# Three of eight feature pairs of the first MLP product by seven block products instead of eight, in chunks 2 to 5

## The chip, the cores and the metric

The kernel runs on one core of a Trainium2 chip. The metric is the device time of one execution in microseconds (us). A core has a matrix engine (TensorE, "PE" in the profile, its weight loads "PEld"), a vector engine (VectorE, "DVE"), a scalar engine (ScalarE, "ACT"), GpSimd ("POOL") and a queue engine for transfers (SyncE, "SP"). Each engine takes its own instructions in order, and they wait for each other by semaphores.

## What is computed

The input is a delta-rule attention over 4 batches, 8 heads, 768 tokens and 48 dimensions per head, followed by an MLP with a SiLU over 3072 tokens of 384 features.

```python
k_n = k / (np.linalg.norm(k, axis=-1, keepdims=True) + 1e-06)
for t in range(S):
    y[:, :, t] = np.einsum('bhd,bhde->bhe', q[:, :, t], state)
    v_old = np.einsum('bhde,bhd->bhe', state, kt)
    state = state + bt[:, :, :, None] * np.einsum('bhd,bhe->bhde', kt, vt - v_old)
...
x = attn_out.transpose(0, 2, 1, 3).reshape(B * S, H * D)
h = x @ w_in                       # 3072x384 by 384x2048
g = h * (1.0 / (1.0 + np.exp(-h)))
return g @ w_out                   # 3072x2048 by 2048x384
```

## The kernel before

The sequence is cut into six chunks of 128 tokens, numbered c = 0 to 5, and each chunk into two halves (hf = 0, 1) of 64 tokens. For each chunk the attention part needs the inverse of a triangular block of 32x32 per head (`invert`, a loop of 31 rank-1 steps on DVE, two instructions each), some small products on PE (`merge`, `keys`, `inner`, `old`, `new`, `update`), and copies by ACT and DVE. The result of a half chunk, transposed, is `xT[c, hf]`: 384 features as three blocks of 128 partitions, by 256 tokens (64 tokens of 4 batches).

For each half chunk the MLP then runs two stages. `hidden` makes the first product: the 2048 hidden features are 16 blocks of 128, taken as eight pairs f = 0 to 7. For one pair, six matmuls of 128x128 weights by 256 tokens fill one bank of PSUM (two feature blocks of 256 tokens, three matmuls accumulating into each), and ACT writes the SiLU of that bank to SBUF (`gT`, L1039, 128x512). The matmuls are in fp32, and every one of them is two MATMUL records and two LDWEIGHTS records in the profile. Two banks, `m0` and `m1`, are used in turn (`bank(M, "phid")`). `combine` makes the second product, in chunks 1 to 5 by seven block products instead of eight, with sums of blocks of `gT` that DVE makes (`sum_g`, L1118), and 192 columns to a matmul (L1136).

The order of the work is written out by hand. The generators `feed_forward(c, hf)` hand out the MLP in small steps, and `run(n)` puts n of these steps between the steps of the attention part; `pin` keeps every engine in the order in which instructions were written. So the PE's queue has matmuls of the MLP between the small products, and DVE's queue has `sum_g` between the rank-1 steps. While `invert(c + 1, ...)` is being written, three of four rank-1 steps are followed by one step of the MLP:

```python
for n, _ in enumerate(invert(c + 1, step)):
    run(int(n % 4 != 3 and n != 24))
```

In chunks 2, 3 and 4 these steps fall on `combine(c, 0)` and `hidden(c, 1)`. In chunk 5 there is no inverse to make for a next chunk. After `invert` come the sums of squares of the chunk after the next (`lengths`, L377, of squares that POOL makes) and the steps of its norms (L391 to L421), still with steps of the MLP between. `hidden` gives a step after three matmuls and one after six, so 16 steps to a half chunk.

Lines that the prediction uses: L1029 the matmuls of the first product, L1039 its SiLU, L1136 those of the second product, L1118 `sum_g`, L615 and L620 the two instructions of a rank-1 step, L623 the scaling at the end of `invert`, L535 a copy by DVE, L532 a copy by ACT, L527 a mask that DVE multiplies onto a score in PSUM, L1144 a scaling by ACT.

Of the kernel before, what the change touches and what calls it, by code (L numbers as in the profile page):

```python
# [10 lines left out]
FP32 = mybir.dt.float32  # L11
U32 = mybir.dt.uint32
ACTF = mybir.ActivationFunctionType
ALU = mybir.AluOpType
# [5 lines left out]
def kernel(  # L20
# [22 lines left out]
    NKT = DM // P  # L43
    NFF = DFF // P
    HB = B // 2
    HH = HB * H
    GT = B * W
    FG = 3
# [55 lines left out]
    def go(steps, n=1):  # L104
        for _ in range(n):
            next(steps, None)
# [9 lines left out]

    kbufs = [const.tile([P, B, NP, 2, W], FP32, name=f"kb{s}") for s in range(2)]
    zbuf = const.tile([P, B, 2, NP, W], FP32, name="z")
    vfs = {}
    LO, HI = slice(0, W), slice(W, P)  # L120
    HALVES = (LO, HI)

    def on(e, hf, g):

        return HALVES[hf ^ e ^ g]

    sums_of_g = const.tile([P, 2, NFF // 2, C], FP32, name="sums_of_g")
# [17 lines left out]
    RUN = C // T * D  # L145
    stage = const.tile([P, B * NP * 2 * C], FP32, name="stage")
# [16 lines left out]
    def in_blocks(c):  # L163

        return 1 < c < NCH
# [7 lines left out]

    def load_k(c, bs=ALL):
        if c < NCH:
            load_pair(kbufs[c % 2], k, c, bs)

    def load_q(c, bs=ALL):
        if c < NCH:
# [25 lines left out]
    for e in range(2):  # L205
        for g in range(2):
            to, of = slice(HH * e + HH // 2 * g, HH * e + HH // 2 * (g + 1)), slice(HH // 2 * g, HH // 2 * (g + 1))
# [6 lines left out]
    w_in = const.tile([P, NKT, DFF], FP32, name="w_in")  # L214
# [83 lines left out]
    def narrow_w_out(i):  # L298
# [14 lines left out]
        out=above[0:W], in_=above[0:W], pattern=[[1, W]], compare_op=ALU.is_gt, fill=0.0,  # L313
# [3 lines left out]
        out=above[W:P], in_=above[W:P], pattern=[[1, W]], compare_op=ALU.is_gt, fill=0.0,  # L317
# [5 lines left out]
    for j in range(NB):  # L323
        rows = slice(T * j, T * (j + 1))
# [36 lines left out]
    def square(c, b):  # L361

        if b == 0:
            sums[c] = small.tile([P, BH], FP32, name="ss", bufs=1)[:]
        if c > 2:
            squared[c, b] = zbuf[:, b].rearrange("p s a w -> p (s a) w")[:, :, 0:D]
        elif b % HB == 0:
            tag = "g" if c > 0 or b > 0 else "x"
            both = work.tile([P, HB, H, D], FP32, name="sq", tag=tag, bufs=1)
            for u in range(HB):  # L370
                squared[c, b + u] = both[:, u]
        kb = kbufs[c % 2][:, b].rearrange("p a e w -> p (a e) w")[:, :, 0:D]
        pin(nc.gpsimd.tensor_tensor(out=squared[c, b], in0=kb, in1=kb, op=ALU.mult))

    def add_squares(c, b):
# [155 lines left out]
    def by_act(to, of):  # L531
        return pin(nc.scalar.copy(to, of))  # L532
# [219 lines left out]
    xTs, parts = {}, {}  # L752
# [88 lines left out]
    def update(c, g, hf):  # L841

        if c == NCH - 1 and hf == 1:
            return
        pu = bank(CC, "pu")
        for u, p, e, n, of, _ in of_heads():
            rows = on(e, hf, g)
            yield pin(nc.tensor.matmul(  # L848
                pu[of, n * D : (n + 1) * D], lhsT=kbufs[c % 2][rows, g * HB + u, p, e, 0:D],
                rhs=zbuf[rows, g * HB + u, hf, p, 0:D], start=True, stop=True,  # L850
            ))
        to = states[g][:, :, :, 0:D]
        pin(nc.vector.tensor_tensor(out=to, in0=to, in1=by_heads(pu), op=ALU.add))
# [160 lines left out]
    gTs = {}  # L1014

    def hidden_of(c, hf, f):

        if (c, hf) == (0, 1):
            return turned_kq[:].rearrange("p b j a t -> p (b j a t)")[:, f * 2 * GT : (f + 1) * 2 * GT]
        return gTs[f // FG][:, f % FG, :]  # L1020

    def hidden(c, hf):

        for f in range(NFF // 2):
            assert ("in", f) in narrowed
            ph = bank(M, "phid")
            for j in range(2):
                for a in range(NKT):
                    pin(nc.tensor.matmul(  # L1029
                        ph[:, j * GT : (j + 1) * GT],  # L1030
                        lhsT=w_in[:, a, (2 * f + j) * P : (2 * f + j + 1) * P],
                        rhs=xTs[c, hf][:, a, :],
                        start=(a == 0), stop=(a == NKT - 1),
                    ))
                if j == 0:
                    yield
            if f % FG == 0 and (c, hf) != (0, 1):
                gTs[f // FG] = mlp.tile([P, FG, 2 * GT], FP32, name="gT", bufs=3)
            pin(nc.scalar.activation(  # L1039
                out=hidden_of(c, hf, f), in_=ph[:], func=ACTF.Silu, scale=-0.5 if in_blocks(c) else 0.5  # L1040
            ))
            if c > 0 and f % FG == 1 and f >= FG:
                for which in (S1, S2):
                    sum_g(which, f // FG - 1)
            yield
# [41 lines left out]
    def sum_w():  # L1087
# [14 lines left out]
    S1, S2, S3, S4 = (  # L1102
        (0, (0, 1), (1, 1), ALU.add), (1, 0, (0, 0), ALU.subtract),
        (0, (0, 0), (0, 1), ALU.subtract), (1, (1, 0), 1, ALU.subtract),
    )

    def group(g):
        return slice(FG * g, min(FG * (g + 1), NFF // 2))

    def sum_g(which, g):  # L1110
        k, left, right, op = which
        fs = group(g)
        of = [
            sums_of_g[:, x, fs] if isinstance(x, int) else
            gTs[g][:, 0 : fs.stop - fs.start, x[0] * GT + x[1] * C : x[0] * GT + (x[1] + 1) * C]
            for x in (left, right)
        ]
        pin(nc.vector.tensor_tensor(out=sums_of_g[:, k, fs], in0=of[0], in1=of[1], op=op))  # L1118
# [251 lines left out]
    def run(n=1):  # L1370

        for _ in range(n):
            name = next(needed, None)
            if name is not None:
                until(name)
            go(pieces)
            begin_soon()
# [121 lines left out]
    for c in range(1, NCH):  # L1499
        if c > 1:  # L1500
            solving = solve(c)
            for n in range(9):
                go(solving)
                run((2, 2, 2, 2, 1, 1, 2, 2, 2)[n])
                if n == 5:
                    pieces = chained(pieces, feed_forward(c, 0), feed_forward(c, 1))
        assert next(solving, 0) == 0
        go(long_2, 99)
        if c + 1 < NCH:
            ready = prepare(c + 1)  # L1510
# [48 lines left out]
```

## Time and profile before

| | us |
|---|---|
| three runs | 653.5, 654.77, 656.47 (median 654.77) |
| the profiled execution | 652.37, its span 650.4 |
| PE busy | 627.6 (96% of the span) |
| DVE busy | 397.6 (61%) |
| ACT busy | 213.8 (33%) |
| POOL busy | 90.9 (14%) |
| mean granted TensorE clock | 0.990 |

A row of the profile names the source line, the engine, the operation, what is written and read, the shapes (partitions x elements) and the count; then the busy time of the group and the mean duration of one, and last the idle time of the engine just before, with what ended it. "Idle time" of PE is counted from the modelled end of one matmul to the start of the next; matmuls overlap in the pipe, so a busy PE may still have lost time, and the distance between the starts of neighbouring matmuls says more than the busy share.

### The profile page before, as it was taken

What the parts mean: (1) busy time and instruction counts of PE and PEld (TensorE: products, weight loads), DVE (VectorE), ACT (ScalarE), POOL (GpSimd) and SP (SyncE); (2) the same over time, 40 slices, a digit from 0 to 9 for tenths busy, and PEclk for the clock granted to TensorE, in tenths of its full rate; (3) what the DMA queues carried; (4) which work ended last, traced back from release to release, by engine and by line L of the source; (5) the groups of instructions that cost most, each with busy time, mean ns of one, the idle gap of its engine ahead of it and who ended that gap; (6) DMA issues with size and microseconds to landing.
All of it is one profiled execution on the core that took longest, in us unless ns stands there. A gap on an engine that the chain in (4) does not pass through costs nothing.

```text
span 650.4 us, 21395 instructions
## 1 busy us (share of the span) xinstructions
PE 627.6 (96%) x9416; PEld 548.0 (84%) x9416; DVE 397.6 (61%) x911; ACT 213.8 (33%) x497; POOL 90.9 (14%) x92
## 2 busy tenths in 40 slices
PE   7878899999989999999999999999999999999997
PEld 5577778756779989989989989989989989889997
DVE  5875689997764987453986453987454974103112
ACT  2455663332342122451122452122451122451111
POOL 5023631334101020010020010020011000000000
PEclk9979999999989999999999999999999999999999
DMA  9876534250288324268324268324173024100101
GB/s 136 209 165 206 192 75 104 98 97 3 53 154 148 58 73 60 50 136 143 59 76 57 48 131 146 61 74 60 28 153 72 10 65 60 40 13 1 25 0 25
DMA packets 145676, 54.70 MB, mean 84 GB/s; under 512 B 117152, under 2 KB 138912, under 8 KB 145584
## 3 DMA queue, kind: packets, MB, share of 16 engines
q1 hardware_dynamic: 143136, 52.93, 39.6%
q8 instruction: 74, 1.21, 0.8%
q10 hardware_dynamic: 2448, 0.41, 0.4%
q14 instruction: 18, 0.15, 0.1%
HBM read 40.14 MB, written 11.01 MB: 79 GB/s over the span
## 4 chain that ended last, share of the span: by engine, by line
PE 91%; DMA 2%; issue 2%; DVE 2%; ACT 1%; SPq 1%; DVEq 0%
PE phid L1029 38%; PE px L1136 16%; PE py L1136 12%; PE po L1064 5%; PE pb_c L828 3%; PE pa L517 2%; PE pb_c L816 2%; PE pyc L907 2%; PE pb_c L1064 2%; PE pb_c L848 1%; PE pb_c L336 1%; PE pyc L894 1%; DMA kb<-in_k_dram 1%; PE pt L488 1%; PE py L770 1%
## 5 line engine op out<-in xcount | busy, mean ns | idle before, releaser
L1029 PE MATMUL phid<-xT,w_in 128*128 128x256 f32 x1152 | 260.1, 383 | 2.1 <-DMA xT<-part 2.0
L1029 PEld LDWEIGHTS phid<-xT,w_in 128*128 128x128 f32 x1152 | 216.9, 191 | 34.4 <-issue 3.0
L1039 ACT ACTIVATE gT<-phid 128x512 f32<-128x512 f32 x88 | 52.5, 597 | 149.8 <-PE phid L1029 145.2
L615 DVE SCALAR_TENSOR_TENSOR rank<-g,step,x 128x31 f32<-128x31 f32 (+15 forms) x124 | 49.8, 401 | 35.8 <-DMA g<-blocks 32.3
L1118 DVE TENSOR_TENSOR sums_of_g<-gT 128x384 f32<-128x384 f32 (+1 forms) x60 | 29.9, 518 | 59.0 <-ACT gT L1039 48.4
L1136 PE MATMUL py<-w_out,sums_of_g 128*128 128x192 f32 x320 | 56.8, 329 | 0.0
L1136 PE MATMUL px<-sums_of_w,sums_of_g 128*128 128x192 f32 x320 | 56.8, 329 | 0.0
L1136 PEld LDWEIGHTS px<-sums_of_w,sums_of_g 128*128 128x128 f32 x320 | 52.2, 190 | 0.5
L1136 PEld LDWEIGHTS py<-w_out,sums_of_g 128*128 128x128 f32 x320 | 52.2, 190 | 0.4
L620 DVE TENSOR_TENSOR x<-x,rank 128x31 f32<-128x31 f32 (+15 forms) x124 | 42.5, 343 | 4.3
L455 POOL TENSOR_TENSOR vf<-vf,n_slot 128x768 f32<-128x768 f32 x10 | 15.0, 1516 | 169.3 <-DMA vf<-in_v_dram 125.3
L476 DVE STREAM_TRANSPOSE kq<-stage 128x512 f32<-128x512 f32 x28 | 28.5, 1114 | 12.0 <-DMA stage<-in_q_dram 10.4
L532 ACT COPY xT<-pyc 48x128 f32<-48x128 f32 (+2 forms) x126 | 32.6, 259 | 1.6
L1136 PE MATMUL px<-sums_of_w,gT 128*128 128x192 f32 x160 | 28.4, 329 | 0.0
L1136 PE MATMUL py<-w_out,gT 128*128 128x192 f32 x160 | 28.4, 329 | 0.0
L1136 PE MATMUL px<-w_out,gT 128*128 128x192 f32 x160 | 28.0, 327 | 0.0
L1136 PEld LDWEIGHTS px<-w_out,gT 128*128 128x128 f32 x160 | 26.4, 190 | 0.5
L538 POOL COPY g<-x 64x256 f32<-64x256 f32 x4 | 5.0, 1241 | 154.5 <-DVE x L623 154.5
L1136 PEld LDWEIGHTS py<-w_out,gT 128*128 128x128 f32 x160 | 26.1, 190 | 0.3
L1136 PEld LDWEIGHTS px<-sums_of_w,gT 128*128 128x128 f32 x160 | 26.1, 190 | 0.2
L828 PEld LDWEIGHTS pb_c<-vf,xi 64*64 64x64 f32 x736 | 23.5, 138 | 3.2 <-issue 2.9
L1147 DVE TENSOR_TENSOR o<-o,kept 128x192 f32<-128x192 f32 (+1 forms) x29 | 11.5, 422 | 24.0 <-ACT kept L1144 24.0
(221 smaller groups left out, 921.6 us busy)
## 6 DMA issues: line engine op xcount, KB each, us to landing
vf<-in_v_dram SPq DMA_DIRECT2D x48, 96.0 KB, 3.2
out_dram<-o SPq DMA_DIRECT2D x42, 96.0 KB, 2.2
w_out<-in_moe_w_in_dram SPq DMA_DIRECT2D x4, 768.0 KB, 4.4
sums_of_w<-in_moe_w_out_dram SPq DMA_DIRECT2D x4, 768.0 KB, 5.9
blocks<-ap SPq DMA_DIRECT2D x44, 64.0 KB, 1.9
g<-blocks SPq DMA_DIRECT2D x5, 512.0 KB, 3.5
kb<-in_k_dram SPq DMA_DIRECT2D x12, 192.0 KB, 5.1
kb<-in_k_dram SPq DMA_DIRECT2D x24, 96.0 KB, 4.6
```

The lines of the kernel that those rows point to most:

```text
L455: pin(nc.gpsimd.tensor_tensor(out=vf, in0=vf, in1=of, op=ALU.mult))
L476: pin(nc.vector.transpose(out=kqs[c, b][:, :, j, :].rearrange("p a (i m) -> p a m i", i=T), in_=src.rearrange("p a (m d) -> p a m d", d=D) ...
L517: pin(nc.tensor.matmul(pa[e][half, p * n * W : (p + 1) * n * W], lhsT=kq[rows, p, 0, half], rhs=kq[rows, p, js[0] : js[-1] + 1, half], sta ...
L532: return pin(nc.scalar.copy(to, of))
L615: pin(nc.vector.scalar_tensor_tensor(out=tv, in0=g[:, 0:m, m : m + 1].to_broadcast([P, m, n]), scalar=step[:, m : m + 1], in1=x[:, m : m + ...
L620: yield pin(nc.vector.tensor_tensor(out=x[:, 0:m, m:T], in0=x[:, 0:m, m:T], in1=tv, op=ALU.add))
L828: yield pin(nc.tensor.matmul(pz[rows, n * D : (n + 1) * D], lhsT=xis[g][rows, u * H + 2 * p + e, :], rhs=vfs[c][rows, hf, g * HB + u, p, : ...
L1029: pin(nc.tensor.matmul(ph[:, j * GT : (j + 1) * GT], lhsT=w_in[:, a, (2 * f + j) * P : (2 * f + j + 1) * P], rhs=xTs[c, hf][:, a, :], star ...
L1039: pin(nc.scalar.activation(out=hidden_of(c, hf, f), in_=ph[:], func=ACTF.Silu, scale=-0.5 if in_blocks(c) else 0.5))
L1064: pin(nc.tensor.matmul(pos[i][:, 0:DM], lhsT=hidden_of(0, hf, f // 2)[:, at : at + C], rhs=w_outs[f // HFF][:, f % HFF, :], start=(f == 0) ...
L1118: pin(nc.vector.tensor_tensor(out=sums_of_g[:, k, fs], in0=of[0], in1=of[1], op=op))
L1136: pin(nc.tensor.matmul(to, lhsT=at, rhs=quarter(f, *b) if isinstance(b, tuple) else sums_of_w[b][:, f], start=start and f == 0, stop=f == ...
```

## The change

It concerns `hidden` for chunks 2 to 5 alone. There, pairs f = 1, 3 and 5 are made by seven block products for eight. A pair has two feature blocks (j = 0, 1), and the 256 tokens are two blocks of 128; over two of the three row blocks (feature blocks a = 0 and 1 of `xT`) this is a 2x2 by 2x2 product of 128x128 blocks, and it is made with seven products of sums of blocks. The third row block (a = 2) is made with four plain products, into which the shared sums are accumulated. That gives eleven matmuls of 128 columns to such a pair, in five groups (`product_steps`: 4, 3, 1, 1 and 2 matmuls), in place of six of 256.

The sums of weight blocks (`w1` to `w4`) are made once, by five DVE instructions in chunk 2 (`sums_of_blocks`), and stay in SBUF. Room for them comes from the tail of `stage` and from the tail of the second key buffer, whose rows are packed without gaps in chunks 3 and 5 (`keys_of`). The sums of token blocks (`x1` to `x5`) are made by four DVE instructions in each half chunk (`add_x`, one of 256 columns and three of 128).

Within a pair by seven, three regions of 128 columns of one PSUM bank, `a`, `b` and `d`, are used: ACT copies `b` and `d` out after the first group, DVE adds `a` to the first of these copies after the second group and ACT copies `d` again, DVE adds `a` again after the third and the fourth group, and after the fifth ACT makes the SiLU of `a` (128 columns) and of the three other blocks (384 columns). Each matmul that follows in `a` accumulates onto what stands there. Between the groups stand matmuls of a plain pair (f + 1), which uses the other bank: one after the first group, two between the second and the third, one between the third and the fourth, one between the fourth and the fifth, one after the fifth.

In the order of the built program, a wait on PSUM goes by bank: the copy of `d` waits for the addition that reads `a`, and the next matmul into `a` waits for that copy; the first matmul of the second group waits for the copy of `b` and `d`. The order on SP and POOL is the same in both programs, and so is the number of steps that `hidden` gives (16).

```diff
+    by_seven = (1, 3, 5)
...
+    def sums_of_blocks():
...
+        a11, a12, a21, a22 = (of(a, j, 0, NS) for j, a in ((0, 0), (0, 1), (1, 0), (1, 1)))
+        pin(nc.vector.scalar_tensor_tensor(
+            out=w1, in0=a21, scalar=-1.0, in1=a22, op0=ALU.mult, op1=ALU.subtract
+        ))
...
+    def hidden_by_seven(c, hf):
...
+        def plain(f):
+
+            ph = bank(M, "phid")
+            for j in range(2):
+                for a in range(NKT):
+                    w = w_in[:, a, (2 * f + j) * P : (2 * f + j + 1) * P]
+                    mm(ph[:, j * GT : (j + 1) * GT], w, xT[:, a, :], a == 0, a == NKT - 1)
+                    yield
+            silu(hidden_of(c, hf, f), ph[:])
+
+        def product_steps(f):
+
+            i = by_seven.index(f)
+            ph, to = bank(M, "phid"), hidden_of(c, hf, f)
+            a, b, d = ph[:, 0:C], ph[:, C : 2 * C], ph[:, 2 * C : 3 * C]
+            at_11, at_22, at_21 = to[:, C : 2 * C], to[:, 2 * C : 3 * C], to[:, 3 * C : 4 * C]
+            mm(d, w3[:, i], x3, start=True)
+            mm(d, w_block(i, 2, 1), x(2, 1))
+            mm(b, w_block(i, 1, 0), x(1, 0))
+            mm(b, w_block(i, 2, 0), x(2, 0), stop=True)
+            by_act(to[:, C : 3 * C], ph[:, C : 3 * C])
+            yield
+            mm(a, w_block(i, 0, 0), x(0, 0))
+            mm(d, w_block(i, 1, 1), x4)
+            mm(d, w_block(i, 2, 1), x5, stop=True)
+            add_x(at_11, a, at_11, ALU.add)
+            by_act(at_21, d)
+            yield
+            mm(a, w2[:, i], x2)
+            add_x(at_21, a, at_21, ALU.add)
+            yield
+            mm(a, w1[:, i], x1)
+            add_x(at_22, a, at_22, ALU.add)
+            yield
+            mm(a, w4(i), x(1, 1))
+            mm(a, w_block(i, 2, 0), x(2, 1), stop=True)
+            silu(to[:, 0:C], a)
+            silu(to[:, C:], to[:, C:])
+            yield
+
+        differ = free[:, 0 : 2 * C].rearrange("p (n t) -> p n t", t=C)
+        first = plain(0)
+        go(first, 3)
+        add_x(differ, xT[:, 0::2, C : 2 * C], xT[:, 0::2, 0:C], ALU.subtract)
+        add_x(x3, x(1, 1), x(0, 1), ALU.subtract)
+        add_x(x2, x(1, 1), x1, ALU.add)
+        add_x(x4, x(1, 0), x2, ALU.subtract)
+        yield
+        go(first, 99)
+        yield
+        for n, f in enumerate(by_seven):
+            by, beside = product_steps(f), plain(f + 1)
+            go(by)
+            go(beside)
+            yield
+            go(by)
+            go(beside)
+            yield
+            go(beside)
+            go(by)
+            go(beside)
+            go(by)
+            yield
+            go(beside)
+            go(by)
+            go(beside, 99)
+            if n == 1:
+                for which in (S1, S2):
+                    sum_g(which, 0)
+            yield
+        last = plain(NFF // 2 - 1)
...
     def hidden(c, hf):
 
+        if in_blocks(c):
+            yield from hidden_by_seven(c, hf)
+            return
...
+                if c == 2 and n == 3:
+                    sums_of_blocks()
```

More of the change, by code (lines that the diff above doesn't have):

```diff
@@ L118, with keys_of @@
     zbuf = const.tile([P, B, 2, NP, W], FP32, name="z")
+    KEPT = B * H * D
+    def keys_of(c):
+        if c % 2 == 0 or c == 1:
+            return kbufs[c % 2]
+        flat = kbufs[1][:].rearrange("p b a e w -> p (b a e w)")
+        return flat[:, 0:KEPT].rearrange("p (b a e d) -> p b a e d", b=B, a=NP, e=2)
     vfs = {}
@@ L175, in load_k @@
         if c < NCH:
-            load_pair(kbufs[c % 2], k, c, bs)
+            load_pair(keys_of(c), k, c, bs)
     def load_q(c, bs=ALL):
@@ L371, in square @@
                 squared[c, b + u] = both[:, u]
-        kb = kbufs[c % 2][:, b].rearrange("p a e w -> p (a e) w")[:, :, 0:D]
+        kb = keys_of(c)[:, b].rearrange("p a e w -> p (a e) w")[:, :, 0:D]
         pin(nc.gpsimd.tensor_tensor(out=squared[c, b], in0=kb, in1=kb, op=ALU.mult))
@@ L848, in update @@
             yield pin(nc.tensor.matmul(
-                pu[of, n * D : (n + 1) * D], lhsT=kbufs[c % 2][rows, g * HB + u, p, e, 0:D],
+                pu[of, n * D : (n + 1) * D], lhsT=keys_of(c)[rows, g * HB + u, p, e, 0:D],
                 rhs=zbuf[rows, g * HB + u, hf, p, 0:D], start=True, stop=True,
@@ L1020, in hidden_of, with blocks_of @@
         return gTs[f // FG][:, f % FG, :]
+    by_seven = (1, 3, 5)
+    NS = len(by_seven)
+    tail = stage[:, B * NP * RUN :]
+    key_tail = kbufs[1][:].rearrange("p b a e w -> p (b a e w)")[:, KEPT:]
+    assert NS * P + P <= B * H * (W - D) and 2 * NS * P + 2 * P <= B * NP * (2 * C - RUN)
+    def blocks_of(t, at, n=NS):
+        return t[:, P * at : P * (at + n)].rearrange("p (n m) -> p n m", m=P)
+    w1, w2, w3 = blocks_of(tail, 0), blocks_of(key_tail, 0), blocks_of(tail, NS)
+    w4s = [blocks_of(tail, 2 * NS, 2), blocks_of(key_tail, NS, 1)]
@@ new lines, in w_block, with of @@
+    def w_block(i, a, j):
+        f = by_seven[i]
+        return w_in[:, a, (2 * f + j) * P : (2 * f + j + 1) * P]
+    def sums_of_blocks():
+        def of(a, j, i, n):
+            span = w_in[:, a, 2 * P : 2 * P + 4 * P * NS].rearrange("p (i q m) -> p i q m", q=4, m=P)
+            return span[:, i : i + n, j]
+        a11, a12, a21, a22 = (of(a, j, 0, NS) for j, a in ((0, 0), (0, 1), (1, 0), (1, 1)))
+        pin(nc.vector.scalar_tensor_tensor(
+            out=w1, in0=a21, scalar=-1.0, in1=a22, op0=ALU.mult, op1=ALU.subtract
+        ))
+        pin(nc.vector.scalar_tensor_tensor(
+            out=w2, in0=w1, scalar=-1.0, in1=a11, op0=ALU.mult, op1=ALU.subtract
+        ))
+        pin(nc.vector.tensor_tensor(out=w3, in0=a11, in1=a21, op=ALU.subtract))
+        at = 0
+        for to in w4s:
+            n = to.shape[1]
+            pin(nc.vector.tensor_tensor(
+                out=to, in0=of(1, 0, at, n), in1=w2[:, at : at + n], op=ALU.subtract
+            ))
+            at += n
@@ new lines, in w4, with x, add_x, mm @@
+    def w4(i):
+        return w4s[0][:, i] if i < 2 else w4s[1][:, i - 2]
+    def hidden_by_seven(c, hf):
+        xT = xTs[c, hf]
+        scale = -0.5
+        for g in (2, 0, 1):
+            gTs[g] = mlp.tile([P, FG, 2 * GT], FP32, name="gT", bufs=3)
+        free = gTs[2][:, FG - 1, :]
+        x1, x5 = free[:, 0:C], free[:, C : 2 * C]
+        x2, x3, x4 = free[:, 2 * C : 3 * C], free[:, 3 * C : 4 * C], sums_of_g[:, 0, NFF // 2 - 1]
+        def x(a, t):
+            return xT[:, a, (1 - t) * C : (2 - t) * C]
+        def add_x(to, a, b, op):
+            pin(nc.vector.tensor_tensor(out=to, in0=a, in1=b, op=op))
+        def mm(to, left, right, start=False, stop=False):
+            pin(nc.tensor.matmul(to, lhsT=left, rhs=right, start=start, stop=stop, skip_group_check=True))
+        def silu(to, of):
+            pin(nc.scalar.activation(out=to, in_=of, func=ACTF.Silu, scale=scale))
+        def plain(f):
[65 more added lines that the diff above has]
+        last = plain(NFF // 2 - 1)
+        go(last, 3)
+        yield
+        go(last, 99)
+        for which in (S1, S2):
+            sum_g(which, 1)
+        yield
@@ L1039, in hidden @@
             pin(nc.scalar.activation(
-                out=hidden_of(c, hf, f), in_=ph[:], func=ACTF.Silu, scale=-0.5 if in_blocks(c) else 0.5
+                out=hidden_of(c, hf, f), in_=ph[:], func=ACTF.Silu, scale=0.5
             ))
```

## The prediction

> **What bounds the kernel now.** I read the head of the page, the busy times and the chain of waits first.
>
> ```profile
> span 650.4 us, 21395 instructions
> ...
> PE 627.6 (96%) x9416; PEld 548.0 (84%) x9416; DVE 397.6 (61%) x911; ACT 213.8 (33%) x497; POOL 90.9 (14%) x92
> ...
> PE 91%; DMA 2%; issue 2%; DVE 2%; ACT 1%; SPq 1%; DVEq 0%
> ...
> L1029 PE MATMUL phid<-xT,w_in 128*128 128x256 f32 x1152 | 260.1, 383 | 2.1 <-DMA xT<-part 2.0
> ```
>
> PE sets the end (91% of the chain), and the first product is its largest group, with 2.1 us of idle time in all. So taking matmul work away pays in full, and a wait that PE did not have costs in full. DVE's 61% is a mean; the timeline of the second half of chunk 2 shows what it hides:
>
> ```profile
> 322.54 20.88 PE L1029 MATMUL phid<-xT,w_in 128*128 128x256 f32 x96
> 343.26 0.98 PE L1136 MATMUL px<-w_out,gT 128*128 128x192 f32 x5
> ...
> 326.16 0.39 DVE L620 TENSOR_TENSOR x<-x,rank 128x220 f32<-128x220 f32 x1
> 334.27 0.83 DVE L535 COPY g<-x 64x768 f32<-64x768 f32 x1
> 339.48 0.18 DVE L391 TENSOR_SCALAR seed<-ss 128x32 uint32<-128x32 uint32 x1
> 343.79 0.77 DVE L411 SCALAR_TENSOR_TENSOR spread<-nr,nt 32x32 f32<-32x32 f32 x4
> ```
>
> PE runs 96 matmul records without a gap, while DVE works through the inverse and the norms. In the written order the copy L535 stands ahead of place 21 of the 48 matmuls of this half and the seed L391 ahead of place 24. At 0.432 us a matmul, PE passed these at 331.6 and 332.9; DVE was through with the two at 335.1 and 339.7. DVE is 3.5 and 6.8 us behind PE, at no cost, since PE needs nothing from DVE there. For the prices:
>
> ```profile
> L620 DVE TENSOR_TENSOR x<-x,rank 128x135 f32<-128x135 f32 x8 | 2.4, 300 | 0.3
> L620 DVE TENSOR_TENSOR x<-x,rank 128x112 f32<-128x112 f32 x8 | 2.2, 275 | 0.3
> L532 ACT COPY ap<-pb_c 128x256 f32<-128x256 f32 x26 | 9.4, 377 | 1.4 <-PE pb_c L517 1.3
> L1144 ACT ACTIVATE kept<-py 128x192 f32<-128x192 f32 x19 | 6.3, 330 | 34.4 <-PE py L1136 34.3
> L527 DVE TENSOR_TENSOR ap<-pa,above 128x256 f32<-128x256 f32 x22 | 9.3, 421 | 14.1 <-ACT ap L532 11.8 <-PE pb_c L517 1.6
> ```
>
> Two timelines show a true wait of PE, and PE's rhythm with 192 columns:
>
> ```profile
> 121.37 0.60 ACT L1039 ACTIVATE kq<-phid 128x512 f32<-128x512 f32 x1 [1.99 <-PE phid L1029]
> 122.02 0.30 PEld L1064 LDWEIGHTS po<-w_out,gT 128*128 128x128 f32 x2 [0.66 <-ACT kq L1039]
> ...
> 304.34 2.76 PE L1136 MATMUL px<-w_out,gT 128*128 128x192 f32 x16
> 306.94 1.30 PE L1136 MATMUL px<-sums_of_w,gT 128*128 128x192 f32 x7
> ```
>
> **The stream on PE.** 96 records of 256 columns take 343.26 - 322.54 = 20.72, so 0.2158 us each; 16 of 192 columns take 2.60, so 0.1625. That is 0.0533 for 64 columns and no more; 128 columns take 0.109, and a matmul (two records) 0.218. A pair by seven takes 11 x 0.218 = 2.40 us instead of 12 x 0.2158 = 2.59. With 24 such pairs (3 x 2 halves x 4 chunks) this gives 24 x 0.19 = 4.6 us, the whole gain. The weight loads: two loads that wait on nothing else start 0.30 - 0.19 = 0.11 apart (122.02), just what a stream of 128 columns covers. The bounds are 0.109 and the row's whole 0.19 a record; at 192 columns the records follow at 0.1625, below 0.19, so I take 0.109.
>
> The Trainium skill speaks against that (TensorE: Matmul & The Clock Gate, "Back-to-back issue gap"): a stream of loads and matmuls at N=128 is measured at about 81 ns, where matmuls alone would take 56. By an estimate from it, 25 ns on each of 22 x 24 records would be 13 us more, were all of them on the path. No run here shows a 128-column stream with such weights yet.
>
> **The five waits of a pair by seven.** PSUM is handed from engine to engine by bank: L527 waits 11.8 us in all for ACT's L532, which only reads the same bank. The Trainium skill has this as a rule (PSUM — Partial Sum Buffer, "PSUM bank collisions raise a hardware error": guard by bank); the trace agrees with these 11.8 us.
>
> A matmul's record is 0.379 for a stream of 0.216, so its result stands 0.163 after its stream, and a reader starts 0.037 later: 0.20. Back, ACT ended at 121.97, PE's load began at 122.02, and the stream with the next load, 0.11 later: 0.16. A DVE addition of 128x128 lies between 0.275 and 0.300, so 0.29; a copy of 256 columns is 0.38, of 128 about 0.26; SiLU of 128 columns, from 0.597 (512) and 0.330 (192), is 0.28. The cover is the plain matmuls between, 0.43 each. So the waits are:
> - after the first group: 0.20 + 0.38 + 0.16 - 0.43 = 0.31. (Part of it may show at the plain pair, whose bank waits for a SiLU queued behind this pair's two; the sum is the same.)
> - after the second: addition, hand-over 0.03, copy: 0.20 + 0.29 + 0.03 + 0.26 + 0.16 - 0.86 = 0.08
> - after the third and the fourth: 0.20 + 0.29 + 0.16 - 0.43 = 0.22 each
> - after the fifth (SiLU, then the next user of the bank): 0.20 + 0.28 + 0.16 - 0.43 = 0.21
>
> Together 1.04 us against 0.19 gained: 0.85 lost in each pair by seven, even where DVE and ACT are free. A pair by seven with its plain pair takes 2.40 + 2.59 + 1.04 = 6.03.
>
> **Where DVE is late.** The additions stand in DVE's order behind the rank-1 steps, and PE now needs them. In the second halves of chunks 2 to 4 PE must go at DVE's pace. DVE's added time in such a half: token sums 0.42 + 3 x 0.29 with hand-overs, 1.4; nine additions at 0.32, 2.9; and between the second and third addition of each pair it waits for PE's matmul, 0.16 + 0.22 + 0.20, three times 1.7. Sum 6.0. After the last addition PE has 0.16 + 0.44 + 0.43 + 0.21 and the last pair 2.59: 3.8.
> - Chunk 2: the last old work ahead of the last addition ended at 344.4 (L411, 343.79 and its first three of four). 344.4 + 6.0 + 3.8 = 354.2, against 343.26: 10.9 later.
> - Chunk 3: that work (L407) ended at 441.5. 451.3 against 439.30: 12.0.
> - Chunk 4: no norms follow. DVE sets the first pair only: old work to 525.2, + 1.4 + 3 x 0.32 + 0.58 = 528.1. Then two pairs at PE's pace, 12.1, and 3.8: 544.0 against 535.38: 8.6.
>
> In the first halves of chunks 2 to 4 the inverse starts after scores that PE makes behind the first pair by seven; so 0.85 shifts DVE too, and what the other two pairs lose is inside DVE's lateness. Chunk 5 has no inverse: six pairs at 0.85.
>
> **The rest.** Token sums in first halves: DVE needs 1.4 us, may begin when `xT` stands, and PE has six plain matmuls (2.6 us) ahead of the first use; nothing. The weight sums: five instructions of 0.57 (L1118 of 128x384), once, 2.9 us of DVE in chunk 2's attention part, where two steps of the MLP (2.6 us) stand before PE needs DVE again; between 0 and 2.9, I take 0 because of these steps. No transfer moves, so nothing on SP or POOL.
>
> **The sum.** 10.9 + 12.0 + 8.6 + 3 x 0.85 + 6 x 0.85 = 39.2 us. The profiled execution took 652.4, of which 650.4 is span: 691.6. It lies 2.4 below the median of the runs, 654.8; against that I forecast 694.
>
> **Rivals.**
> - It gains: every wait is covered and only the stream counts, 654.8 - 4.6 = 650.2. This needs the chains of 0.65 us after the third and fourth group to fit into 0.43, so an addition with both hand-overs in 0.27 less what PE's pipe takes. For it: a plain matmul or two stand beside every group. Against it: the wait at 122.02 shows the full 0.05 + 0.11 of the way back. 4%.
> - Within 0.5%: stream gain and waits cancel, a loss under 0.33 a pair. 2%.
> - The five waits alone, DVE's lateness swallowed somewhere: 24 x 0.85 = 20.4, 675. For it: DVE idles 8 us a chunk before the inverse (32.3 us for `g` in its rows). Against it: this wait is for a transfer that starts no earlier. 20%, with all that lies between.
> - My forecast, 685 to 702: 56%.
> - Worse: nothing is absorbed, 39.2 + 6 x 0.85 + 2.9 = 47.2, 702. 10%.
> - Weight loads not hidden: with 0.19 for each record, 22 x 0.081 = 1.8 us on each pair that PE paces, (6 + 3 + 2) x 1.8 = 20 more, 714. 8%. The rule of the TensorE page above would make it 11 x 0.55 = 6 more, 700, by estimate.
>
> The range is 675 to 704. A difference under 0.5% (3.3 us) can hardly be told from none here. Faster 4%, same 2%, slower 94%.
>
> **What the profile after would show.** Records of 128 columns 0.109 apart inside a group; about 0.2 us of idle time at PE's loads ended by the DVE additions and by ACT; and in the second halves of chunks 2 to 4, `hidden` lasting some 30 us instead of 20.7, with the longest waits of PE ended by DVE. In chunk 5 it should last 2.5 us longer. I am wrong if a pair by seven with its plain pair takes under 5.2 us in chunk 5, or if the second halves there and in chunk 3 last equally long.

## The result, and the profile after

The changed kernel takes 704.97 us (median of 6 runs, 699.9 to 705.73), the kernel before 654.13 (6 runs, 651.95 to 660.95). The ratio is 1.074, with an interval of 1.068 to 1.080. The forecast was 694, with a range of 675 to 704: slower, as forecast, but by 50.8 us where the sum said 39.2, and 1 us above the upper end of the range. Ratios leave out runs in the chip's slower state, which are one of the ten runs of the first experiment and one of the thirteen of the kernel before beside it.

The profiled execution after took 705.32, its span 703.4, 53.0 more than before. The page after, lines of its head, busy times, chain and groups:

```profile
span 703.4 us, 22066 instructions
...
PE 656.4 (93%) x9656; PEld 548.1 (78%) x9656; DVE 425.4 (60%) x1020; ACT 229.7 (33%) x569; POOL 90.7 (13%) x92
...
PE 64%; DVE 17%; SPq 5%; DMA 4%; issue 4%; ACT 4%; POOL 1%; POOLq 0%; DVEq 0%; ACTq 0%
...
L1090 PE MATMUL phid<-xT,w_in 128*128 128x256 f32 (+1 forms) x720 | 164.2, 355 | 6.1 <-ACT gT L541 3.0
...
L1087 DVE TENSOR_TENSOR gT<-phid,gT 128x128 f32<-128x128 f32 x72 | 20.9, 290 | 76.3 <-PE phid L1090 76.2
```

L1090 is the first product of chunks 2 to 5 (L1029 before), L1087 the 128x128 additions, L1093 the SiLU, L541 ACT's copies. PE's share of the chain fell from 91% to 64%, and DVE's rose from 2% to 17%: PE no longer sets the end everywhere. What PE's weight loads waited for, over the whole span (us in total, times, longest):

```profile
PEld phid L1090 <- ACT gT L541: 27.1, 43, 2.5
PEld phid L1090 <- DVE gT L1087: 23.0, 47, 2.9
PEld phid L1090 <- ACT gT L1093: 11.3, 25, 1.8
```

These are 61.4 us of idle time at the loads; before, the loads of the first product waited for nothing of the kind. They overlap with matmuls still in the pipe, so the price is read from the distance between two marks instead: from the first matmul of a half chunk's first product to the first matmul of its second product.

| first product of | before | after | more | forecast |
|---|---|---|---|---|
| chunk 2, first half | 25.18 | 29.80 | 4.63 | 0.85 |
| chunk 2, second half | 20.72 | 30.93 | 10.20 | 10.9 |
| chunk 3, first half | 27.08 | 30.72 | 3.64 | 0.85 |
| chunk 3, second half | 20.72 | 31.36 | 10.64 | 12.0 |
| chunk 4, first half | 27.18 | 32.44 | 5.26 | 0.85 |
| chunk 4, second half | 20.72 | 27.02 | 6.30 | 8.6 |
| chunk 5, first half | 26.08 | 30.59 | 4.51 | 2.55 |
| chunk 5, second half | 20.72 | 23.56 | 2.84 | 2.55 |

The sum is 48.0, and the fastest runs of the two kernels lie as far apart (699.9 and 651.95). The second products beside them last as long as before (18.20 in first halves). The rest of the 53.0 lies almost all ahead of anything that was changed. The two lines below are the windows view of before and of after, from the start to the first matmul of the MLP (us, busy time and count of PE, weight loads, DVE, ACT and POOL, granted clock, DMA share, GB/s):

```profile
0.00:52.30 52.30, 42.47 (x1022) 32.44 (x1022) 37.68 (x106) 22.75 (x50) 16.48 (x30) 0.90 0.83 167
```

```profile
0.00:57.50 57.50, 46.01 (x1023) 34.82 (x1023) 37.64 (x106) 22.95 (x50) 16.53 (x30) 0.82 0.84 164
```

The work is the same, and the granted clock is 0.90 in one and 0.82 in the other. In the traces of the experiments this start lasted from 51.92 (a form of the changed kernel) to 59.08 (a form of the kernel before), so its 5.1 us here are no sign of the change. Single profiled executions are therefore compared by the marks in what follows, not by their ends.

### The profile page after: what moved, and what is told of

It is laid out like the page before. It is cut to its first block, busy times and chain, and to the rows that moved or that the text cites. A ratio compares the mean times of both kernels' runs of the same rounds, so it can differ in the third digit from the quotient of the medians.

```text
span 703.4 us, 22066 instructions
## 1 busy us (share of the span) xinstructions
PE 656.4 (93%) x9656; PEld 548.1 (78%) x9656; DVE 425.4 (60%) x1020; ACT 229.7 (33%) x569; POOL 90.7 (13%) x92
## 4 chain that ended last, share of the span: by engine, by line
PE 64%; DVE 17%; SPq 5%; DMA 4%; issue 4%; ACT 4%; POOL 1%; POOLq 0%; DVEq 0%; ACTq 0%
PE phid L1090 20%; PE px L1290 10%; PE py L1290 6%; PE phid L1183 6%; DVE rank L624 5%; DVE x L629 5%; PE po L1218 5%; PE pb_c L837 2%; PE pb_c L345 2%; DVE sums_of_g L1272 2%; SPq L896 2%; SPq L167 2%; ACT xT L541 2%; PE pa L526 2%; PE pb_c L1218 1%
## 5 line engine op out<-in xcount | busy, mean ns | idle before, releaser
L1090 PE MATMUL phid<-xT,w_in 128*128 128x256 f32 (+1 forms) x720 | 164.2, 355 | 6.1 <-ACT gT L541 3.0
L1090 PEld LDWEIGHTS phid<-xT,w_in 128*128 128x128 f32 x720 | 111.4, 194 | 24.5 <-ACT gT L541 11.8
L1183 PE MATMUL phid<-xT,w_in 128*128 128x256 f32 x384 | 89.9, 389 | 0.2 <-DMA xT<-part 0.2
L1183 PEld LDWEIGHTS phid<-xT,w_in 128*128 128x128 f32 x384 | 72.5, 193 | 11.5 <-DMA xT<-part 0.6
L1087 DVE TENSOR_TENSOR gT<-phid,gT 128x128 f32<-128x128 f32 x72 | 20.9, 290 | 76.3 <-PE phid L1090 76.2
L1093 ACT ACTIVATE gT<-phid 128x512 f32<-128x512 f32 x64 | 30.4, 475 | 92.8 <-PE phid L1090 90.5
L1090 PEld LDWEIGHTS phid<-gT,stage 128*128 128x128 f32 x96 | 15.1, 193 | 24.7 <-DVE gT L1087 15.2
L541 ACT COPY xT<-pyc 48x128 f32<-48x128 f32 (+2 forms) x126 | 32.7, 260 | 1.6
L1090 PE MATMUL phid<-gT,stage 128*128 128x128 f32 x96 | 23.4, 326 | 9.7 <-DVE gT L1087 9.7
L541 ACT COPY gT<-phid 128x256 f32<-128x256 f32 (+1 forms) x48 | 15.3, 319 | 49.2 <-DVE gT L1087 37.8
```

What stands on the lines that cost most here:

```text
L1087: pin(nc.vector.tensor_tensor(out=to, in0=a, in1=b, op=op))
L1090: pin(nc.tensor.matmul(to, lhsT=left, rhs=right, start=start, stop=stop, skip_group_check=True))
L1093: pin(nc.scalar.activation(out=to, in_=of, func=ACTF.Silu, scale=scale))
L1183: pin(nc.tensor.matmul(ph[:, j * GT : (j + 1) * GT], lhsT=w_in[:, a, (2 * f + j) * P : (2 * f + j + 1) * P], rhs=xTs[c, hf][:, a, :], star ...
```

## The experiments

The theory after the result: the five waits stand as priced; DVE's lateness makes the second halves of chunks 2 to 4 long; and first halves lose more than 0.85 a pair by seven because the additions and copies stand in the queues of DVE and ACT behind the attention part's work. The rivals: weight loads that 128 columns do not cover; the first halves' loss shifting work so that the second halves lose less; and DVE's own work rather than its waiting.

**The stream without the waits.** Nothing is read between the groups, and the sums of tokens and of partial products are left out, so that the eleven matmuls run with plain inputs (this kernel does not compute the MLP).

```diff
-            mm(b, w_block(i, 2, 0), x(2, 0), stop=True)
-            by_act(to[:, C : 3 * C], ph[:, C : 3 * C])
-            yield
+            mm(b, w_block(i, 2, 0), x(2, 0))
             mm(a, w_block(i, 0, 0), x(0, 0))
...
-            add_x(at_11, a, at_11, ALU.add)
-            by_act(at_21, d)
...
-            add_x(at_21, a, at_21, ALU.add)
...
-            add_x(at_22, a, at_22, ALU.add)
```

> Every pair by seven keeps its eleven matmuls of 128 columns, but nothing reads the bank between them and the sums of token blocks are left out (plain blocks are multiplied in their place; one SiLU of 384 and one of 128 columns at the end, then the plain pair), so the output is not that of the MLP. If the loss comes from the reads between the groups and 128-column matmuls follow at 0.109 us, all 24 pairs gain their 0.19: 4.6 us less than before, about 649 to 650, and a half chunk's first product takes 20.72 - 0.57 = 20.15 in chunk 5's second half. If weight loads don't hide behind 128 columns, each pair costs up to 1.8 more: up to 690, and that half up to 25.5.

Measured: 656.44 (10 runs), ratio 1.001 (0.997 to 1.005), where 649 to 650 was expected. Every second half's first product is 0.40 shorter than before (20.32 instead of 20.72), so 0.13 a pair instead of 0.19. From the timeline of this kernel on PE, one pair by seven and its plain pair, to the start of the next:

```profile
612.25 0.38 PE L1090 MATMUL phid<-xT,stage 128*128 128x128 f32 x2
...
617.29 0.38 PE L1090 MATMUL phid<-xT,stage 128*128 128x128 f32 x2
```

That is 5.04, less 12 records of 0.2158 is 2.45 for 22 records: 0.111 each. So 128 columns do cover their weight loads, and the rival of uncovered loads (0.19 a record) falls. The whole gain to be had is 8 x 0.40 = 3.2 us, 0.5% of the time, and even this does not show in the sum: the second products of chunks 2 and 3, beside the solve of the attention part, took 1.3 and 3.2 longer in the profiled execution, and the first half of chunk 5 came out 0.64 longer. In these two second products PE waits for a transfer of the solve, `xe<-low`, for which it does not wait before. What its loads waited for, in chunk 2 and in chunk 3:

```profile
PEld py L779 <- DMA xe<-low: 1.2, 2, 0.6
```

```profile
PEld py L779 <- DMA xe<-low: 1.8, 2, 1.1
```

In chunk 3 a stretch of 3.41 us at half clock (a granted clock of 0.50) comes on top, at 443.2; the last section has more on these. So PE arrives earlier and waits there instead. That the inverse on DVE, from which this transfer comes, sets its time was not tested. In chunk 5 it is 0.7 us of idle time that the profile ties to no engine.

**First halves alone, second halves alone.** The other halves are made as before.

```diff
-        if in_blocks(c):
+        if in_blocks(c) and hf == 0:
             yield from hidden_by_seven(c, hf)
...
```

(and `hf == 1` in the other kernel. The halves made as before get back the factor of their SiLU.)

> By seven in the first halves (hf = 0) of chunks 2 to 5 alone. If what a half loses stays lost, as the changed kernel's marks say, the first products of these halves lose 4.6, 3.6, 5.3 and 4.5: 18 us over before, with the second halves back at 20.72. By my prediction's price (five waits alone, 0.85 a pair) it would be 12 x 0.85 = 10.

> By seven in the second halves (hf = 1) of chunks 2 to 5 alone. My prediction: 10.9, 12.0, 8.6 and 2.6 longer, 34 us over before, because without the first halves' waits PE arrives earlier and finds DVE that much later. If instead the losses of the two halves simply add, it is what these halves lost in the changed kernel: 10.2 + 10.6 + 6.3 + 2.8 = 30.

First halves alone: 670.79 (4 runs), ratio 1.024 (1.017 to 1.032); the marks of chunks 2 to 5 give +7.17, +3.61, +5.27 and +3.00, and every second half stays at 20.72. Second halves alone: 686.0 (4 runs), ratio 1.045 (1.040 to 1.049); +10.59, +12.99, +6.43 and +2.84, and no first half gets longer. The ratios add up, 2.4% and 4.5% against 7.4%. So the first halves cost 16.5 us by the medians and 19.05 by the marks (2.5 of these from a stretch at half clock, last section), and not the 10.2 of twelve pairs at 0.85. Whether some of that is absorbed by the second halves can be told only roughly. By the medians nothing is (16.5 + 31.7 = 48.2 us alone, 50.8 together). By the marks the second halves lose 32.85 alone and 29.98 beside the first, so at most 2.9 is absorbed; 2.35 of it is in chunk 3, whose second half, alone, also had two stretches at half clock instead of one.

**Without the inverse.** In the inverses of chunks 2 to 5 each of the 31 rank-1 steps works on one element instead of up to 256, so the inverse is not computed; all instructions, waits and their order stay. The same edit to the kernel before is the control.

```diff
-            n = T - m
+            n, k = (1, 1) if c > 1 else (T - m, m)
...
-                out=x[:, 0:m, m:T], in0=x[:, 0:m, m:T], in1=tv, op=ALU.add
+                out=x[:, 0:k, m : m + n], in0=x[:, 0:k, m : m + n], in1=tv, op=ALU.add
```

> The changed kernel with the rank-1 steps of the inverses of chunks 2 to 5 cut to one column by one row (both instructions stay, at some 0.19 us instead of 0.20 to 0.48; the inverse is not computed). If DVE's lateness behind these steps makes the second halves of chunks 2 to 4 long, they fall from 30.9, 31.4 and 27.0 to about 23.6, as in chunk 5: 18 us less than the changed kernel, about 682 to 687. If it is not DVE, nothing changes: 700 to 705.

> The kernel before with the same cut of the inverses (not computed). Its PE needs nothing of DVE early in these halves, so all that I hold says the same time as before, 652 to 656; a kernel that is bound by DVE there would gain.

The control: 653.66 (8 runs), ratio 1.0005 (0.997 to 1.004), all first products unchanged; before, DVE's inverse cost nothing. The changed kernel without it: 691.11 (4 runs), ratio 1.053 (1.047 to 1.059), some 14 us less than the changed kernel and above the 682 to 687 that were expected. The second halves fall to 27.22, 28.17 and 23.81; chunk 4 then costs about as much as chunk 5 (23.56), as DVE's lateness would have it. Chunks 2 and 3 keep some 4 us too much. The timeline of DVE in this kernel, second half of chunk 2, shows on what:

```profile
344.50 0.29 DVE L1087 TENSOR_TENSOR gT<-phid,gT 128x128 f32<-128x128 f32 x1 [0.89 <-PE phid L1090]
345.04 0.55 DVE L386 TENSOR_REDUCE ss<-z 128x8 f32<-128x384 f32 x1 [0.25 <-POOL z L382]
345.82 0.55 DVE L386 TENSOR_REDUCE ss<-z 128x8 f32<-128x384 f32 x1 [0.23 <-POOL z L382]
346.60 0.55 DVE L386 TENSOR_REDUCE ss<-z 128x8 f32<-128x384 f32 x1 [0.23 <-POOL z L382]
347.39 0.55 DVE L386 TENSOR_REDUCE ss<-z 128x8 f32<-128x384 f32 x1 [0.23 <-POOL z L382]
347.97 0.18 DVE L400 TENSOR_SCALAR seed<-ss 128x32 uint32<-128x32 uint32 x1
348.07 0.28 DVE L1087 TENSOR_TENSOR gT<-phid,gT 128x128 f32<-128x128 f32 x1
```

DVE goes at GpSimd's pace through the sums of squares for the norms of the chunk after the next, and the next addition, for which PE waits, stands behind all four.

**Without GpSimd's squares as well.** DVE reads the keys instead of GpSimd's squares, with instructions of the same size, so the norms of chunks 4 and 5 are not computed; the inverse is left out as above.

```diff
+        if c > 3:
+            squared[c, b] = kb
+            return
         pin(nc.gpsimd.tensor_tensor(out=squared[c, b], in0=kb, in1=kb, op=ALU.mult))
...
```

> The changed kernel with the inverse left out, and in addition the squares by which GpSimd feeds the norms of chunks 4 and 5: the sums of squares on DVE become maxima of the keys themselves, of the same size, so DVE has the same work there and no wait for GpSimd (the norms of chunks 4 and 5 are then wrong). With the inverse alone left out the first products of the second halves took 27.22 us in chunk 2, 28.17 in chunk 3, 23.81 in chunk 4 and 23.56 in chunk 5. There DVE stood four times some 0.23 us for GpSimd's squares, an addition behind each block of them, and 3.2 us of squares could start only when the scaling and a copy were done. Theory (what is left of the lateness in chunks 2 and 3 is DVE standing in line for GpSimd's squares): 24 to 25.5 in both. Rival (it is DVE's own work for the norms, some 20 small instructions, 6 us): 27 to 28 as before. The first halves and chunk 4 stay as they were, 23.8 in chunk 4.

The second halves of chunks 2 and 3 took 24.65 and 25.74, chunk 4 23.82 (one run). The first halves stayed, but for chunk 2: 32.51 instead of 29.82, with a stretch of 6.8 us at half clock at 286.2. The same place in this kernel, DVE's timeline:

```profile
341.11 0.29 DVE L1090 TENSOR_TENSOR gT<-phid,gT 128x128 f32<-128x128 f32 x1 [0.90 <-PE phid L1093]
341.32 1.92 DVE L389 TENSOR_REDUCE ss<-kb 128x8 f32<-128x384 f32 x4
343.28 0.18 DVE L403 TENSOR_SCALAR seed<-ss 128x32 uint32<-128x32 uint32 x1
343.37 0.28 DVE L1090 TENSOR_TENSOR gT<-phid,gT 128x128 f32<-128x128 f32 x1
```

Between the two additions lie 2.26 us instead of 3.57. So some 2.5 of the 4 us in either half came of standing in line for GpSimd (with a slower clock that followed such waits there, below, and that is gone here as well), and 1.1 and 2.2 are left, which DVE's own work would explain; no run takes that work away. The first theory takes it: 24 to 25.5 was expected, 25.74 is a little above.

**More cover beside each pair by seven.** In the second half of chunk 5 alone, two pairs by seven instead of three, each beside two plain pairs, for which a third bank is free there; behind the first four groups stand 2, 3, 2 and 2 plain matmuls.

```diff
+        if (c, hf) == (NCH - 1, 1):
+            for n, (f, g, h) in enumerate(((1, 2, 4), (5, 3, 6))):
+                by, beside = product_steps(f), chained(plain(g), plain(h, A))
+                for cover in (2, 3, 2, 2):
+                    go(by)
+                    go(beside, cover)
...
```

> In the second half of chunk 5 alone, two pairs by seven (1 and 5) in place of three, each beside two plain pairs, one of them in a third bank: 2, 3, 2, 2 and 3 plain matmuls stand behind the five groups instead of 1, 2, 1, 1, 1. The chains behind the groups (0.74, 1.01, 0.65, 0.65, 0.64 us) then fit under 0.86, 1.30, 0.86, 0.86, 1.30. If the waits are chain less cover, that half's first product takes 20.72 - 2 x 0.19 = 20.34, at most 20.6 with the start, instead of 23.56. If a read of the bank costs PE something that cover doesn't hide, it stays over 20.72: two pairs at 1.08 - 0.19 each make 22.5. The whole time hardly shows it: 3 us less than the changed kernel.

696.18 (2 runs), ratio 1.068 (1.055 to 1.081). The half took 20.56 instead of 23.56, 0.16 less than before, and the table of waits has no wait of PE's loads for this half. So with every wait covered the 2.84 are gone, and the waits account for them: three pairs at 1.08 of waits (below) less 0.13 of gain make 2.85.

**Two banks for one pair.** In the same half, `b` and `d` lie in a bank of their own.

```diff
+            pd = bank(A, "phid") if (c, hf) == (NCH - 1, 1) else ph
-            a, b, d = ph[:, 0:C], ph[:, C : 2 * C], ph[:, 2 * C : 3 * C]
+            a, b, d = ph[:, 0:C], pd[:, C : 2 * C], pd[:, 2 * C : 3 * C]
...
```

> In the second half of chunk 5 alone, b and d lie in a bank of their own (a third one), a in the other. If waits go by bank, the second group's first matmul no longer waits for the copy, the copy of d no longer waits for the addition, and the next pair's first group no longer waits for the SiLU of a; the plain pair's bank then waits 0.43 for its SiLU, and 0.22 stay behind the third and fourth group each. That half's first product takes 22.8 instead of 23.56. If the waits follow the data alone, it stays at 23.56.

700.96 (2 runs), ratio 1.075 (1.065 to 1.086); the half took 22.55, +1.83. What PE's loads waited for in this half, in the changed kernel and then with two banks:

```profile
PEld phid L1090 <- DVE gT L1087: 2.1, 6, 0.4
PEld phid L1090 <- ACT gT L541: 2.0, 6, 0.4
PEld phid L1090 <- ACT gT L1093: 1.0, 3, 0.3
```

```profile
PEld phid L1090 <- DVE gT L1087: 2.3, 6, 0.4
PEld phid L1090 <- ACT gT L1093: 0.3, 1, 0.3
```

The two waits of each pair for ACT's copies go, though the matmul that waited writes `a`, which the copies do not read: they were the bank's. Two of the three waits for the SiLU go with them. The Trainium skill's rule of guarding by bank (PSUM — Partial Sum Buffer, "PSUM bank collisions raise a hardware error") is what the program's waits follow here, at a measured 1.0 us for three pairs (23.56 against 22.55).

**The copies by DVE in first halves.**

```diff
-            by_act(to[:, C : 3 * C], ph[:, C : 3 * C])
+            (by_act if hf else by_dve)(to[:, C : 3 * C], ph[:, C : 3 * C])
...
-            by_act(at_21, d)
+            (by_act if hf else by_dve)(at_21, d)
```

> The changed kernel, but in first halves the copies of b and d of each pair by seven (128x256 and 128x128) are made by DVE instead of ACT. In the changed kernel the first half of chunk 5 took 30.59 us, 4.51 more than before, of which three pairs at 0.95 explain 2.84; one wait there lasted 1.18 instead of 0.15, for ACT's 128x128 copy, in whose queue stood one copy of 0.58 and six of 0.27 of the attention part, while DVE had been idle for 7.4. Theory (the excess of the first halves is ACT's queue): chunk 5 gives back about 1.0, to 29.3 to 29.8; in chunks 3 and 4, where the waits for ACT's copies are 0.7 and 1.5 + 0.5, 0.5 to 1.8 come back if DVE is free, and it gets longer than 30.72 and 32.44 if DVE itself is late there. Rival (the excess is the matmuls of the attention part on PE, or PSUM): chunk 5 stays at 30.6 or gets longer by the slower copies. Second halves unchanged (30.93, 31.36, 27.02, 23.56).

One run. The first halves took 28.32, 30.00, 30.90 and 29.99 in chunks 2 to 5: 1.48, 0.72, 1.54 and 0.60 less, 4.3 in all. This is clear of the scatter: in the five other traces with these first halves and the second halves by seven they took at least 29.79, 30.68, 32.10 and 30.54. Of the second halves, which were to stay, two did (31.37 and 23.56); chunk 2 took 29.66, 1.27 less, for a reason that stays open, and chunk 4 28.39, 1.37 more (last section). ACT's timeline in the first half of chunk 5, first of the changed kernel, where PE's load at 622.08 waits for the 128x128 copy, then with the copies on DVE:

```profile
619.53 0.58 ACT L541 COPY part<-pyc 48x512 f32<-48x512 f32 x1 [1.27 <-PE pyc L916]
620.12 1.62 ACT L541 COPY xT<-pyc 48x128 f32<-48x128 f32 x6
621.77 0.27 ACT L541 COPY gT<-phid 128x128 f32<-128x128 f32 x1
```

```profile
606.87 0.58 ACT L541 COPY part<-pyc 48x512 f32<-48x512 f32 x1 [1.94 <-PE pyc L916]
607.46 1.62 ACT L541 COPY xT<-pyc 48x128 f32<-48x128 f32 x6
609.10 0.58 ACT L541 COPY part<-pyc 48x512 f32<-48x512 f32 x1
609.71 1.62 ACT L541 COPY xT<-pyc 48x128 f32<-48x128 f32 x6
611.35 0.28 ACT L1093 ACTIVATE gT<-phid 128x128 f32<-128x128 f32 x1
```

In the first, the copy of `d` stands behind 2.2 us of the attention part's copies. In the second, that wait is gone, and the SiLU after the fifth group stands behind 4.4 us of them instead; PE's wait for it is 0.82 in place of 0.20. So chunk 5 gave back 0.6 and not the expected 0.8 to 1.3: the queue was the cause, and part of the wait moved to the next instruction in it.

No version here that computes the MLP beats the kernel before. The best half (0.16 shorter, with more cover) saves 0.02% of the time.

## Why the prediction was right and wrong

**The stream: right, the gain a little smaller.** 0.109 a record was taken, 0.111 measured; 0.13 gained a pair, not 0.19. The Trainium skill's 25 ns more at N=128 (TensorE: Matmul & The Clock Gate, "Back-to-back issue gap") does not show in these fp32 matmuls; by it, 0.134 would have stood there, by estimate.

**The five waits: right.** Gaps in PE's stream in the second half of chunk 5, from the ends of the records less the pipe's 0.163 and the stream: 0.29, 0.15, 0.22, 0.22 and 0.20, together 1.08, where 0.31, 0.08, 0.22, 0.22 and 0.21 were worked out, 1.04. The timeline of PE's weight loads shows them in the order third, fourth, fifth, first and second, after the second of the pair before (the bracket counts from the end of the load before, so it is larger than the gap):

```profile
663.84 0.30 PEld L1090 LDWEIGHTS phid<-gT,kb 128*128 128x128 f32 x2 [0.29 <-ACT gT L541]
...
664.71 0.30 PEld L1090 LDWEIGHTS phid<-gT,stage 128*128 128x128 f32 x2 [0.35 <-DVE gT L1087]
...
665.59 0.30 PEld L1090 LDWEIGHTS phid<-xT,stage 128*128 128x128 f32 x2 [0.35 <-DVE gT L1087]
...
666.66 0.30 PEld L1090 LDWEIGHTS phid<-gT,stage 128*128 128x128 f32 x2 [0.33 <-ACT gT L1093]
...
668.28 0.30 PEld L1090 LDWEIGHTS phid<-xT,w_in 128*128 128x128 f32 x2 [0.42 <-ACT gT L541]
...
669.97 0.30 PEld L1090 LDWEIGHTS phid<-gT,kb 128*128 128x128 f32 x2 [0.29 <-ACT gT L541]
```

From 663.84 to 669.97 the period is 6.13, where 6.03 was forecast. Each pair by seven costs 2.84 / 3 = 0.95 where both queues are free, not 0.85.

**DVE's lateness: right in kind, 4.4 too long.** The second halves of chunks 2 to 4 were to lose 10.9, 12.0 and 8.6 and lost 10.2, 10.6 and 6.3; without the inverse chunk 4 loses 3.1. Chunks 5 and 3 do differ, 23.6 against 31.4. In chunk 4 the term was mis-sized in DVE's old work: the step of 128x156 was set at 10.5 after the half's start, and ended there at 9.9 although some 1.4 us of additions and token sums stood ahead of it in the half. The rank-1 step of 128x256 began 1.6 before the half's first matmul, where it had begun 0.2 after it. With second halves alone it began 1.4 before it as well, so it is not the first halves alone that give DVE this lead. What moved is the start of the inverse: its first step, which waits for the transfer `g<-blocks`, stood 15.4 ahead of the half's first matmul in the kernel before, 17.0 with second halves alone and 19.9 in the changed kernel. The forecast kept DVE's old distance to PE. Why the transfer stands earlier was not taken apart.

**The first halves: wrong.** The step that failed is the price of 0.85 a pair, which was worked out for free queues and used where ACT and DVE have the attention part's work, together with "what the other two pairs lose is inside DVE's lateness". The forecast had 3 x 0.85 + 2.55 = 5.1; measured were 18.0. Of these, 12 x 0.95 = 11.4 are the waits of twelve pairs at the price measured in the second half of chunk 5; at most 2.9 of the 18.0 was absorbed, where the forecast had six pairs inside DVE's lateness. Of the other 6.6, 4.3 come back when the copies leave ACT's queue. The rest was not taken apart; it holds waits for DVE's additions (one of 1.19 in chunk 4) and, in chunk 5, 0.7 of idle time that the profile ties to no engine and that the kernel before does not have. PE's waits for transfers of `xT` there are 1.3 in both kernels and explain nothing.

**The sum.** 39.2 was 8.8 under the 48.0 of the marks: 12.9 too little for first halves, 4.1 too much for second halves. That the total came within a fifth is thus partly luck, since the two errors have opposite signs. The weight sums at nothing were nearly right: the attention part in which they stand lasted 0.3 longer (30.96 against 30.63).

**The rivals.** A gain and a tie fall with the first table, the weight loads with the stream alone. "The five waits alone, 20.4" is the 8 x 2.84 = 22.7 that the marks contain, but neither DVE's lateness nor ACT's was swallowed. Nearest came "nothing is absorbed", 47.2 against the 48.0 of the marks, and this is partly luck: its six pairs did show in first halves, but its 2.9 for the weight sums did not come, and it has neither the 6.6 of queues nor the 4.1 too much for second halves.

## What to carry to other kernels

A change that trades PE work for reads between matmuls is priced twice: once with free engines, here 0.2 us out of PE and 0.16 back, and once by what stands in the reading engine's queue at that place in the written order. An engine that is late at no cost, or busy at 33%, has a price as soon as PE waits for something behind its work. An arithmetic saving of one product in eight (one in twelve of a pair's matmuls here) pays only if other matmuls stand behind every group whose result is read before PE goes on; here chains of 0.64 to 1.01 us had to be covered, and 0.86 to 1.30 us of matmuls covered them.

## What the runs showed that was not expected

A wait of PE has an echo in its clock. In the second half of chunk 2 of the changed kernel PE stood for 2.53 us until 351.48; the windows view of after shows the stretch that followed, with 3.4 us on either side of it, with the granted clock in the third column from the right:

```profile
348.49:351.89 3.40, 0.87 (x6) 0.47 (x5) 2.21 (x6) 0.00 (x0) 1.94 (x3) 1.00 0.65 213
351.89:355.30 3.41, 3.41 (x14) 2.89 (x13) 2.99 (x13) 1.29 (x3) 0.00 (x0) 0.50 1.05 156
355.30:358.71 3.41, 3.38 (x21) 2.43 (x19) 1.74 (x9) 0.64 (x2) 0.00 (x0) 1.00 1.21 114
```

For 3.41 us the clock was 0.50. The length of a pause does not decide this alone. In the eleven traces of this case, from 70 us on, such a stretch began between 0.4 us before and 1.8 us after the end of 11 of 13 pauses of PE of 2.0 us or more, and of 8 of 42 pauses between 1.2 and 2.0; two stretches have no such pause ahead of them.

The traces show what does fit. In each trace, all such stretches begin a whole number of 3.413 us apart, so they stand on a grid, which lies differently in each execution. Cut along this grid, 21 windows from 70 us on, not at half clock themselves, have PE busy for 51% or less, and 20 of them were followed by half clock; of the other 1900 one was (at 60%). Two windows with the same program and the same two pauses of 1.15 and 1.28, in the second half of chunk 4, show it (the first number behind the length is PE's busy time). With the copies by DVE in first halves, then in the changed kernel:

```profile
547.63:551.04 3.41, 1.67 (x8) 1.04 (x8) 2.65 (x10) 0.27 (x1) 0.00 (x0) 1.00 0.01 2
551.04:554.45 3.41, 3.41 (x14) 3.06 (x14) 2.30 (x9) 1.29 (x3) 0.00 (x0) 0.50 0.00 0
```

```profile
560.10:563.51 3.41, 1.97 (x10) 1.12 (x8) 3.17 (x10) 0.27 (x1) 0.00 (x0) 1.00 0.00 0
563.51:566.93 3.42, 2.43 (x14) 1.75 (x15) 2.67 (x9) 0.81 (x3) 0.00 (x0) 1.00 0.00 0
```

In the first, the window holds the whole second pause and 0.46 of the first, PE is busy for 49% of it, and the next window is at 0.50. In the second, it holds the whole first pause and 0.29 of the second, PE is busy for 58%, and the clock stays. So by these traces the share of a window in which PE is idle goes with the half clock, and luck in the phase decides which execution pays. PE's busy time is modelled, and no run set this share on purpose, so the cause is not shown.

A stretch costs up to half of its length where PE sets the pace: the half of chunk 4 took 28.39 with it and 27.02 without, and a stretch of 6.8 us in the first half of chunk 2 made it 32.35 with first halves alone, instead of 29.80. The Trainium skill (TensorE: Matmul & The Clock Gate, "HAM oscillation — how this bites in real kernels") warns of idle gaps over about 3.4 us; here 1.74 us of idle time in a window of 3.41, from two pauses, were followed by half clock. The forecast had no such term.
